# A fused gated-attention and feed-forward kernel: another order of its first loads, and one unit's transposes moved to the matrix engine

## The chip, the cores and the metric

The kernel runs on one core of a Trainium2 chip. Its engines work side by side, each through its own list of instructions in order: TensorE (PE in the profile; PEld is its weight load), VectorE (DVE), ScalarE (ACT), GpSimd (POOL) and SyncE (SP, which here only issues transfers). Transfers of all queues share 16 DMA engines. The metric is the device time of one execution in microseconds.

## The reference, cut to what matters

```python
B, H, S, D = q.shape                       # 4, 8, 768, 48
f = 1.0 / (1.0 + np.exp(-f_logit))
for t in range(S):
    state = f[:, :, t, :, None] * state + einsum('bhd,bhe->bhde', k[:, :, t], v[:, :, t])
    y[:, :, t] = einsum('bhd,bhde->bhe', q[:, :, t], state)
x = y.transpose(0, 2, 1, 3).reshape(B * S, H * D)      # 3072 x 384
h = x @ w_in                                            # w_in 384 x 2048
out = (0.5 * h * (1.0 + erf(h / sqrt(2)))) @ w_out      # w_out 2048 x 384
```

A recurrence with a decay for each channel is followed by a feed-forward layer with a gelu. Inputs and result are float32.

## The kernel before, in words

**Tiling.** The 3072 tokens are 24 tiles of 128. Two neighbouring tiles make a unit (u = 0 to 11, counted from zero: the "third unit" is u = 2, the "seventh" is u = 6) and also a group of the feed-forward part. Units 0 to 4 (`PAIRS`) hold tokens in an interleaved way and are called pair units; the others are natural ones.

**A unit's work.** Its logits (f), keys (k), values (v) and queries (q) are loaded by SyncE. ACT turns the logits to log decays (E at L494, L at L497), PE sums them over time (L521 to L527, L515), ACT takes exponentials of the sums (RG at L543, GT at L549, GL at L565 or L570), DVE or GpSimd multiplies keys and queries by them (L576), and the values are cast (VC, L583). Then keys and queries must be turned, that is transposed (`turn`, L592): either by PE with an identity matrix (L611) and a copy out of PSUM (L617), or, for units in `KDMA`, by two DMA transposes that SyncE issues (L599). PE makes the scores (L722 or L784), DVE masks them (L631), PE forms the state update (L745 or L806), which is carried on by DVE and GpSimd (L651 to L662), and the outputs (L699, L705, L758, L826). These are cast (L675) and turned (L691 or, for `XDMA`, by DMA at L679) to be the left side of the feed-forward part.

**A group's feed-forward work.** F1 (L875): eight steps of six matmuls of 256 columns with w_in, each step into one PSUM bank; ACT applies the gelu to each (L885). F2 (L896): for each tile 16 matmuls of 384 columns with w_out, in four quarters r = 0 to 3, each of which needs its piece of w_out and four of the group's gelu blocks; all 16 add up in one PSUM bank. The four banks of this pool (`s_fh`) serve F1 and F2 alike. A copy (L901) and a store (L906) follow; the last tile is split in halves (L917, L921).

**Weights.** w_in comes in three pieces, i0 (1024 columns, which steps 0 to 3 use), i1 (512, steps 4 and 5) and i2 (512, steps 6 and 7). w_out comes in four, o0 to o3, one for each quarter of F2. GpSimd issues them (L461, L464), as they are cast to bfloat16 on the way.

**Tables.** ACT holds one table for the exponentials and logarithms and another for the gelu. Each change loads a table (L953).

**Order.** Nothing in the order is left to a compiler. `Plan.run` lays all operations out with assumed durations; each has a priority, to which it adds a random number drawn from a seed of its unit (`SEEDS`). Every engine then runs its instructions in the planned order. The order of loads is the list `LOADS`. When the issuing engine changes from one entry to the next, a gate is put in: the transfer waits until an earlier one of the other kind has landed, the second back in the list for a SyncE load and the fourth back for a GpSimd load (or the next further back of that kind). The lines are

```python
        if i and order[i - 1][0] != eng:
            back = 4 if eng == "pool" else 2
            for j in range(i - back, -1, -1):
                if order[j][0] != eng:
                    gate = order[j][1]
                    break
```

While PE waits early in the plan, dummy matmuls on a tile of zeros fill the planned gaps (L947, junk).

Of the kernel before, what the change touches and what calls it, by code (L numbers as in the profile page):

```python
# [24 lines left out]

SPREAD, SEED = (1.0, 97)

SEEDS = [1643, 41, 3215, 1275, 2533, 2502, 823, 887, 1264, 763, 2447, 3095]

NUDGE = {}  # L30
XA = 0.0
# [53 lines left out]
class Plan:  # L85
# [30 lines left out]
    def run(self):  # L116
        free = dict.fromkeys(list(LAT), 0.7)
        free["DMA"] = 1.8
        rng = random.Random(SEED)
        own = [random.Random(x) for x in SEEDS]  # L120
        for o in self.ops:
            if o.prio > -5:
                k = min(max(int(o.prio % 1000) // 20, 0), len(SEEDS) - 1)
                o.prio += rng.uniform(-SPREAD, SPREAD)
                if SEEDS[k]:
                    w = (0.5, 1.0, 3.0, 8.0)[SEEDS[k] % 4]
                    o.prio += own[k].uniform(-w, w)
# [98 lines left out]
GAM = []  # L226
ODVE = [0, 1, 2, 4, 6, 7, 8, 9, 10, 11, 12, 13, 14, 16, 17, 18, 19, 20, 21, 22, 23]
XDMA = [5, 6, 7, 8, 9, 10, 11]
KDMA = [4, 5, 6, 7, 8, 9, 10, 11]
AJ = [2, 3, 4, 5, 6, 7, 8, 10, 11]  # L230
NGT = 4
GLD = []
G1D = [2, 3, 4]
YJ = [2, 3, 4]
ROWS = [16, 17, 18, 19]
AMX = []
WARM = 30.0
LOADS = ['f0', 'k0', 'v0', 'q0', 'f1', 'v1', 'k1', 'q1', 'i0', 'k2', 'f2', 'v2', 'q2', 'i1', 'i2', 'i3', 'o0', 'o1', 'o3', 'o2', 'f3', 'k3', 'q3', 'u4', 'v3']
LOADS += [f"u{n}" for n in range(12) if f"u{n}" not in LOADS and f"c{2 * n}" not in LOADS and f"f{n}" not in LOADS]


@with_exitstack
def kernel(
# [185 lines left out]
    wo_src = moe_w_out.rearrange("(r p j) m -> r p j m", r=4, j=4)  # L429
    for what in LOADS:  # L430
        m = int(what[1:])
# [160 lines left out]
    def turn(u, kq):  # L592


        for j in range(2):
            n = 2 * u + j
            sc = X[n]["sc"]
            if u in KDMA:
                P.add("DMA", 1.5, lambda sc=sc, j=j: nc.sync.dma_start_transpose(  # L599
# [256 lines left out]
    def ffn_group(g):  # L856
# [31 lines left out]
        for s_ in range(s):  # L888
# [14 lines left out]
            def store(n=n, osb=osb):  # L903
                w = C // 2 if n in ROWS else C
                for r in range(0, C, w):
                    nc.sync.dma_start(out=out[n * C + r:n * C + r + w, :], in_=osb.t()[r:r + w, :])  # L906
# [80 lines left out]
```

## Time and profile before

| | |
|---|---|
| Time, median of 3 runs | 182.77 us (182.22 to 183.18) |
| Span of the profiled run | 181.1 us |
| PE busy | 171.7 us, 95% |
| ACT busy | 125.2 us, 69%, of which 15 table loads take 19.2 |
| DVE busy | 96.3 us, 53% |
| GpSimd busy | 53.6 us, 30% |
| DMA | 32.61 MB, mean 180 GB/s |
| Largest groups | F1 (L875) 68.7 us, F2 (L896) 66.0, gelu (L885) 57.5 |

Busy time is the union of an engine's instructions. [...] Idle time of an engine matters only if the engine that sets the end waits for it.

### The profile page before, as it was taken

The numbers are of one execution on the slowest core, as the hardware profiler recorded it, in microseconds if no ns is written. First come the engines' busy times: TensorE is split into PE (matmuls) and PEld (weight loads), VectorE is DVE, ScalarE is ACT, GpSimd is POOL, SyncE is SP. The second block draws the span as 40 slices with busy tenths as digits, with TensorE's granted clock in tenths as the row PEclk, the third lists the DMA queues.
The fourth block names the chain that finished last, engine by engine and source line by source line (L and its number), as shares of the span: only waits on it lengthen the run. The fifth ranks groups of instructions, "written<-read, shape, count | busy, mean of one in ns | idle before, by whom it ended". The sixth has DMA issues, their size and how long they took to land.

```text
span 181.1 us, 4916 instructions
## 1 busy us (share of the span) xinstructions
PE 171.7 (95%) x1990; PEld 132.3 (73%) x1990; DVE 96.3 (53%) x194; ACT 125.2 (69%) x212; POOL 53.6 (30%) x116
## 2 busy tenths in 40 slices
PE   7788889999999999988999999999999999999993
PEld 2356669966787688785779689976697986886972
DVE  5289750058898564244896692527691625362110
ACT  2775198963899189999967759777585578560720
POOL 7657870003043641140176113112435110300000
PEclk9999999999999999999999999999999999999999
DMA  6999999949997898999999999999999872814102
GB/s 148 261 261 226 268 170 203 200 115 267 278 266 142 186 197 170 249 227 171 216 179 213 215 175 207 195 187 189 185 245 181 181 162 47 166 37 91 43 0 87
DMA packets 106998, 32.61 MB, mean 180 GB/s; under 512 B 102113, under 2 KB 106081, under 8 KB 106977
## 3 DMA queue, kind: packets, MB, share of 16 engines
q1 hardware_dynamic: 105056, 29.07, 79.7%
q0 software_dynamic: 1776, 3.15, 9.8%
q8 instruction: 15, 0.25, 0.6%
q10 hardware_dynamic: 144, 0.10, 0.2%
q14 instruction: 7, 0.05, 0.1%
HBM read 25.17 MB, written 4.72 MB: 165 GB/s over the span
## 4 chain that ended last, share of the span: by engine, by line
PE 64%; ACT 15%; DMA 15%; SPq 3%; issue 1%; DVE 0%; DVEq 0%
PE ps L875 26%; PE ps L896 25%; ACT gT L885 7%; DMA fl<-in_f_logit_dram 7%; DMA win<-in_moe_w_in_dram 5%; ACT L953 4%; SPq L449 3%; DMA kq<-sc 2%; PE ps L722 2%; PE ps L758 2%; PE ps L917 1%; ACT gt L549 1%; PE ps L521 1%; PE ps L699 1%; PE ps L745 1%
## 5 line engine op out<-in xcount | busy, mean ns | idle before, releaser
L885 ACT ACTIVATE gT<-ps 128x512 bf16<-128x512 f32 x96 | 57.5, 671 | 24.6 <-PE ps L875 23.0
L875 PE MATMUL ps<-xT,win 128*128 128x256 bf16 x576 | 68.7, 273 | 1.3 <-ACT gT L885 0.9
L896 PE MATMUL ps<-wout,gT 128*128 128x384 bf16 x368 | 66.0, 326 | 0.0
L875 PEld LDWEIGHTS <-win 128*128 128x128 bf16 x576 | 61.6, 114 | 3.9 <-issue 1.2
L896 PEld LDWEIGHTS <-gT 128*128 128x128 bf16 x368 | 34.2, 98 | 19.5
L583 POOL CAST vb<-vt 128x384 bf16<-128x384 f32 x22 | 12.6, 584 | 52.5 <-DMA vt<-in_v_dram 52.4
L631 DVE TENSOR_TENSOR am<-ps,mask 128x512 bf16<-128x512 f32 x28 | 17.6, 684 | 15.1 <-PE ps L722 15.1
L901 DVE COPY osb<-ps 128x384 f32<-128x384 f32 x20 | 11.1, 556 | 25.9 <-PE ps L896 18.2
L657 POOL TENSOR_TENSOR tn<-rr,gl 128x384 f32<-128x384 f32 x16 | 14.0, 872 | 35.2 <-DVE rr L655 34.6
L576 DVE TENSOR_TENSOR sc<-qt,gt 128x384 bf16<-128x384 f32 x23 | 14.0, 616 | 13.7 <-ACT gt L549 13.7
L576 DVE TENSOR_TENSOR sc<-kt,rg 128x384 bf16<-128x384 f32 x23 | 13.5, 597 | 11.3 <-ACT rg L543 11.3
L953 ACT ACT_TABLE_LOAD x15 | 19.2, 1283 | 0.3
L662 POOL CAST sb<-tn 48x192 bf16<-48x192 f32 x40 | 14.8, 371 | 11.6 <-DVE tn L651 6.6
L494 ACT ACTIVATE fl<-fl 128x768 f32<-128x768 f32 x12 | 10.1, 842 | 10.5 <-DMA fl<-in_f_logit_dram 10.5
L675 DVE CAST yb<-ps 128x384 bf16<-128x384 f32 x22 | 11.9, 555 | 7.4 <-PE ps L758 3.7
L631 DVE TENSOR_TENSOR am<-ps,maskp 128x512 bf16<-128x512 f32 x20 | 12.5, 684 | 2.2 <-PE ps L784 1.4
L543 ACT ACTIVATE rg<-ps 128x384 f32<-128x384 f32 x21 | 10.3, 503 | 4.4 <-PE ps L523 2.8
L549 ACT ACTIVATE gt<-ps 128x384 f32<-128x384 f32 x21 | 10.2, 503 | 3.9 <-PE ps L523 3.3
L947 PE MATMUL ps<-junk 128*128 128x512 bf16 (+3 forms) x36 | 10.4, 423 | 2.1 <-POOL junk L939 1.3
L655 DVE TENSOR_TENSOR rr<-ps,tn 128x384 f32<-128x384 f32 x16 | 8.9, 553 | 3.5 <-POOL tn L657 1.8
L497 ACT ACTIVATE lf<-fl 128x768 bf16<-128x768 f32 x12 | 10.1, 843 | 0.4
L947 PEld LDWEIGHTS <-junk 128*128 128x128 bf16 x36 | 3.6, 111 | 6.2 <-issue 3.5
(74 smaller groups left out, 130.4 us busy)
## 6 DMA issues: line engine op xcount, KB each, us to landing
out_dram<-osb SPq DMA_DIRECT2D x19, 192.0 KB, 3.1
fl<-in_f_logit_dram SPq DMA_DIRECT2D x14, 192.0 KB, 3.8
kt<-in_k_dram SPq DMA_DIRECT2D x14, 192.0 KB, 3.8
qt<-in_q_dram SPq DMA_DIRECT2D x14, 192.0 KB, 3.7
vt<-in_v_dram SPq DMA_DIRECT2D x14, 192.0 KB, 3.9
fl<-in_f_logit_dram SPq DMA_DIRECT2D x5, 384.0 KB, 6.2
kt<-in_k_dram SPq DMA_DIRECT2D x5, 384.0 KB, 6.2
vt<-in_v_dram SPq DMA_DIRECT2D x5, 384.0 KB, 5.7
```

The lines of the kernel that those rows point to most:

```text
L549: P.add("ACT", 0.40, lambda g=gps[j], gtv=gtv: nc.scalar.activation(gtv(), g.t()[:, 0:HD].rearrange("q (p h d) -> q p h d", h=2, d=D), AF. ...
L576: P.add("POOL" if pl else "DVE", 0.80 if pl else 0.475, lambda a=a, y=y, j=j, w=w, pl=pl, b=(gtv if w else rg): (nc.gpsimd if pl else nc.v ...
L583: P.add("ACT" if hv else "POOL", 0.40 if hv else 0.47, lambda y=y, j=j, hv=hv: (nc.scalar.copy if hv else nc.gpsimd.tensor_copy)(y["vb"].t ...
L631: P.add("POOL" if pl else "DVE", 1.15 if pl else 0.61, lambda hh=hh, pl=pl: (nc.gpsimd if pl else nc.vector).tensor_tensor(ams[hh].t(), ap ...
L657: P.add("POOL", 0.83, lambda: nc.gpsimd.tensor_tensor(tn.t(), rr.t(), glb(), ALU.mult), rd=[("rr", n), ("gl", n)], wr=[("tn", n)], bufs=[r ...
L662: P.add("POOL", 0.36, lambda hh=hh: nc.gpsimd.tensor_copy(sb.t()[64 * hh:64 * hh + D, :, D * hh:D * hh + D], tn.t()[64 * hh:64 * hh + D, : ...
L675: P.add("ACT" if help_ else "DVE", 0.40 if help_ else 0.475, lambda: copier(help_)(yb.t()[:, i, :], yp.t()[:, 0:HD]), rd=[("yp", n)], wr=[ ...
L875: nc.tensor.matmul(hps.t()[:, i * tok:(i + 1) * tok].rearrange("a (s t) -> a s t", s=s), col(fo)[:, kk, :], xT.t()[:, :, kk, :], start=(kk ...
L885: nc.scalar.activation(to, fr, AF.Gelu)
L896: nc.tensor.matmul(op.t()[:, 0:d_model], gT.t()[:, fo, s_ * C:(s_ + 1) * C], wout[fo // 4][:, fo % 4, :], start=(fo == 0), stop=(fo == FO ...
L947: nc.tensor.matmul(o.opens.t()[:, 0:w], junk[:, 0:C], junk[:, 0:w], start=True, stop=True, skip_group_check=True)
L953: nc.scalar.preload_act_table_set({"exp": "natural_log_exp_and_others", "gelu": "gelu_and_others"}[o.table])
```

## The change

Three lists of the schedule change and all seeds are drawn anew.

- `LOADS`: the third unit's logits (f2) go ahead of w_in; of w_in the last piece (i2) comes first, then i0, and i1 only after o0 and o1. By the rule of gates i2 then waits for v1, k2 for i2, and o0 for f2. Before, i0 waited for f1, i1 for k2, and k2 for nothing. (The entry i3 names no piece and does nothing.)
- `KDMA`: the seventh unit leaves the list, so PE turns it, with DVE's copies.
- `ROWS`: stores of tiles 14 and 15 are split in two halves.
- `SEEDS`: twelve new numbers.

It is meant to have the third unit's decays at hand before ACT turns to gelus, to let F1 start on a smaller piece of w_in, and to take a latency of two DMA transposes from the seventh unit.

```diff
-SEEDS = [1643, 41, 3215, 1275, 2533, 2502, 823, 887, 1264, 763, 2447, 3095]
+SEEDS = [2199, 3779, 3998, 3287, 1370, 1237, 3921, 2695, 3442, 2008, 790, 3051]
...
-KDMA = [4, 5, 6, 7, 8, 9, 10, 11]
+KDMA = [4, 5, 7, 8, 9, 10, 11]
...
-ROWS = [16, 17, 18, 19]
+ROWS = [14, 15, 16, 17, 18, 19]
...
-LOADS = ['f0', 'k0', 'v0', 'q0', 'f1', 'v1', 'k1', 'q1', 'i0', 'k2', 'f2', 'v2', 'q2', 'i1', 'i2', 'i3', 'o0', 'o1', 'o3', 'o2', 'f3', 'k3', 'q3', 'u4', 'v3']
+LOADS = ['f0', 'k0', 'v0', 'q0', 'f1', 'v1', 'k1', 'q1', 'f2', 'i2', 'i0', 'k2', 'v2', 'q2', 'i3', 'o0', 'o1', 'i1', 'o3', 'o2', 'f3', 'k3', 'q3', 'u4', 'v3']
```

## The prediction

> **What bounds the kernel now.** I read the page's busy line first, then busy time by stretch, the chain, and at last ACT and the DMA queues before 60 us.
>
> ```profile
> PE 171.7 (95%) x1990; PEld 132.3 (73%) x1990; DVE 96.3 (53%) x194; ACT 125.2 (69%) x212; POOL 53.6 (30%) x116
> ```
>
> PE is the bound, but a busy PE need not be a fast one, so I count its work. The chain gives prices where PE runs back to back:
>
> ```profile
> 97.55 0.55 PE ps L722 x16
> 108.62 5.89 PE ps L875 x54
> 119.23 3.90 PE ps L896 x24
> ```
>
> A logit-side product of the feed-forward part (F1, L875) costs 5.89/54 = 0.109 us, one of its second half (F2, L896) 3.90/24 = 0.1625, a natural unit's scores (L722) 0.55. The busy time by stretch gives the room:
>
> ```profile
> 20.60:28.60 8.00, 7.13 (x105) 5.98 (x106) 3.37 (x7) 5.51 (x7) 5.28 (x10) 1.00 1.14 198
> 28.60:50.00 21.40, 21.40 (x261) 16.41 (x259) 10.34 (x21) 16.36 (x28) 1.50 (x3) 1.00 0.99 215
> 50.00:60.00 10.00, 9.55 (x167) 7.96 (x166) 8.31 (x16) 9.30 (x18) 4.83 (x9) 1.00 0.86 197
> 75.00:85.00 10.00, 9.06 (x81) 6.72 (x80) 4.09 (x8) 9.93 (x17) 2.64 (x5) 1.00 1.14 209
> 85.00:178.10 93.10, 93.06 (x962) 74.33 (x960) 49.10 (x90) 62.18 (x111) 20.22 (x37) 1.00 0.81 156
> ```
>
> Columns: length, then busy us and count of PE, PEld, DVE, ACT, POOL. The same view for single lines gives counts to multiply:
> - 20.6 to 28.6: 36 F1 = 3.9, attention pieces of the chain 2.0, together 5.9 of 8.0: 2.1 us of slack (1.13 of it is filled by five junk matmuls, L947).
> - 50 to 60: 48 F1 = 5.2, 7 F2 = 1.1, attention 2.7: 9.0 of 10, slack 1.0.
> - 75 to 85: 36 F1 = 3.9, 25 F2 = 4.1, scores and state 0.7: 8.7 of 10, slack 1.3. ACT is full there (9.93).
> - 85 to 178.1: 336 F1 = 36.6, 246 F2 = 40.0, the split last tile (L917) 2.65, attention 12.5: 91.8 of 93.1.
>
> So the second half is packed: added PE work lengthens it, and only slack before 85 us can be won, some 4.4 us. Where it comes from:
>
> ```profile
> 10.84 9.78 DMA win<-in_moe_w_in_dram
> 20.67 2.16 PE ps L875 x18
> 28.86 7.43 ACT gT L885 x12
> 36.31 1.28 ACT L953
> 40.33 6.34 DMA fl<-in_f_logit_dram
> 52.96 1.28 ACT L953
> ```
>
> F1 starts when the first w_in piece lands (20.6). From 25.6 to 36.3 ACT does 16 gelus; only after a table change at 36.31 does it make unit 2's exponentials. Unit 3 and 4 then wait for loads that SyncE issues from 37.75 on, as it waits for w_out (o3): 16.8 us in the waits of SP. The DMA view of 35.5 to 38.5 has only 0.15 MB in 3 us.
>
> ```profile
> 22.56 0.84 ACT L494 ACTIVATE fl<-fl 128x768 f32<-128x768 f32 x1 [3.89 <-DMA fl<-in_f_logit_dram]
> 24.30 1.28 ACT L953 ACT_TABLE_LOAD   x1
> 37.60 0.49 ACT L549 ACTIVATE gt<-ps 128x384 f32<-128x384 f32 x1
> ```
>
> Unit 2's logits came at 22.5, 10.8 us after issue. In the DMA view of 15 to 19 the reason stands:
>
> ```profile
> q0 software_dynamic: 340, 0.68, 90.1%
> q1 hardware_dynamic: 370, 0.14, 20.0%
> ```
>
> While weights flow (q0), 170 KB/us are theirs and 35 are left to the inputs (q1), which alone get 1.31 MB in 5 us = 262 KB/us (8 to 13).
>
> **What the Trainium skill says.** "DMA: Bandwidth & Descriptors", section Queues, rings and completion order: an engine turns between its queues packet by packet. That agrees: about equal counts (340, 370), so the queue with bigger packets takes the bandwidth. "ScalarE: Activation LUTs", section What ACT_TABLE_LOAD costs: 1283 ns for any set, and a drain of 1380 more. The trace has 1283 each, 15 times; the drain isn't seen (the load at 24.30 ends 0.01 before the gelu). "TensorE: Matmul & The Clock Gate", Part 4: a 128x128 bf16 transpose takes some 275 ns in context, and needs a copy from PSUM. Here it takes 219 (L611), pipelined: eight weight loads in 0.45 us.
>
> **The change, part by part.**
>
> *Loads.* Nothing is added or dropped; order and gates change. The first w_in transfer (now i2, 384 KB) waits for v1 rather than f1. f1 landed at 10.55; 384 KB at 262 KB/us is 1.5 us, so v1 is at 12.1, q1 at 15.0. Before, i0 was issued at 10.84 and, by 0.1 MB outside 15 to 19, began to flow at about 14.3: 3.5 later. So i2 flows from 15.6 (estimate). By then f2, now behind q1, has 0.6 us x 262 = 157 KB; 227 are left. At 35 KB/us that ends after the whole of i2 and i0 (1152 KB, 6.4 us at 180), at 22; with twice that share while i2 flows (its packets are half as long) it lands at 20.4. Bounds: 16.5 (no contention) and 22.5. I take 20.4, only 2 us earlier than before. i2 lands about 18.8, i0 about 23.2 (before 20.6).
>
> The sense of it is on ACT: unit 2's E and L (1.7), sums (0.7), exponentials (1.9, from 37.6 to 39.4 plus a wait for the subtraction) can all precede the gelus, then one table load 1.28: gelus start at 20.4 + 5.6 = 26.0 against 25.6. PE in 18 to 26 has 12 F1 from i2 and 12 from i0 until its four PSUM banks are full, as before. So +0.4; the junk block of 1.13 us need not recur, take -0.4: sum 0. With the bounds -2.0 (f2 at 18) and +2 (f2 at 22.5).
>
> A pair of table loads goes (36.31, and one around it): 2.6 us of ACT, worth something only where ACT limits.
>
> *Added waits.* k2 on SP now waits for i2 (18.8), with v2 and q2 queued behind it. o0 on GpSimd waits for f2; behind it stand o1, i1, then unit 1's state work and unit 2's v casts. After 22 the inputs get some 262 KB/us for a microsecond and then a trickle under o0, o1, i1 (1152 KB, to about 29): q2 lands near 31.5 rather than 25.7. Its products ran at 38.1 to 39.1, so this lateness is hidden by the gelus. Unit 2 then turns near 32 to 34, 5 us earlier. i1 at about 30 feeds the last F1 of both groups while 12 gelus are still to do: hidden. F2 needs o2 at the end of its sum, about 38.5 (before 39.5); meanwhile 36 F1, early F2 quarters and unit 2 keep PE full.
>
> o3 follows the v casts: about 36.3, so f3 goes out 1 to 1.5 us sooner, and unit 2's tokens are at hand for F1 by 43 rather than 51. Hence the slack of 50 to 60 should go: -1.0. That of 75 to 85 (ACT full, a key transpose by DMA awaited at 83.4 and 84.1) should shrink by most: -1.2, bounds 0 and -1.3.
>
> *Seventh unit by TensorE.* Removes 2 of 16 DMA transposes (1.25 us of SP issue and 3.4 to landing each) and adds 16 transposes on PE: 16/8 x 0.45 = 0.9 us, and two DVE copies of 0.68. DVE is 84% busy in 90 to 100 but has 40 us to spare after it; its copies lie beside F1 and F2. PE is packed there: +0.9 in full. Before, unit 6's scores (97.55) met no wait of PE, so little comes back. SP is free 2.5 us sooner for loads: hidden.
>
> *Rows and seeds.* Stores of tiles 14 and 15 in halves: two more issues near 125 us, out of buffers' way, 0. The seeds reshuffle priorities in every unit. They alter no work; where PE is packed, order costs nothing. Their part is in the slack before 85: no price in the trace, I take 0, bounds +-1.
>
> Sum: 0 - 1.0 - 1.2 + 0.9 = -1.3: 182.8 - 1.3 = 181.5.
>
> **Rivals.**
> - *Slower, weights starve the rest.* f2 lands at 22.5 as now; five microseconds of exponentials stand before the first gelu, so gelus start at 28. PE loses about 1.3 of its 5.9 us of work before 28.6; unit 6 adds 0.9; the later slack shrinks by only 0.3: 182.8 + 1.9 = 184.7. For it: the 170 to 35 split, and weights that come as one queue. Against it: f2 has a head start, and PE had F1 to do.
> - *No change.* Only one of the two later slacks goes (-1.0), against 0.9: 182.7. For it: the packed second half makes unit 6's cost sure.
> - *Much faster.* f2 is through before the weights flow (18 or less), gelus start at 23.6, two more microseconds are won in the first stretch: 179.5. Against it: my 227 KB left at 15.6.
>
> **How the numbers follow.** Forecast 181.5 (0.42), much faster 179.5 (0.13), no change 182.7 (0.17), slower 184.7 (0.28). The limit of 0.5% is 0.9 us: faster, below 181.9, takes the first two, 0.55; same 0.17; slower, above 183.7, 0.28. The range leaves out a tenth at each side: 179.4 (half of much faster) to 184.9 (the starved case with a further loss by seeds left out).
>
> **What would show it.** Right: 14 or fewer table loads; no exponentials of unit 2 after the first gelus; f2's activation before 21.5; gelus from about 26; PE's count in 50 to 60 and 75 to 85 up by a microsecond of work; L611 at 80 instructions; SP's transposes of kq at 14. Wrong: gelus from 28 or later; a PE gap between 20 and 30 of over 3 us; f3 issued after 38; scores of unit 6 waiting for a DVE copy; a stretch after 85 with PE under 99%.

## The result, and the profile after

The changed kernel takes 189.5 us (median of 6 runs, 188.46 to 191.29) against 182.63: 1.0368 times as long, 95% interval 1.0315 to 1.0421. Some executions of a kernel fall in a slower state (one of these six, 191.29): the ratios, and the times in the table of experiments, leave them out. The span of the profiled run grew from 181.1 to 187.7 us. The page's busy line of PE and the group of table loads, after:

```profile
PE 174.6 (93%) x2002; PEld 133.9 (71%) x2002; DVE 100.2 (53%) x196; ACT 130.7 (70%) x216; POOL 52.6 (28%) x116
L953 ACT ACT_TABLE_LOAD x19 | 24.4, 1283 | 0.3
```

PE is busy for a smaller share, and table loads rose from 15 to 19 where 14 or fewer were forecast. Busy time by stretch, after (length, then PE, PEld, DVE, ACT, POOL, the granted PE clock, DMA share, GB/s; the granted clock is the share of its full speed at which PE was allowed to run):

```profile
20.00:25.00 5.00, 5.00 (x88) 3.19 (x88) 3.74 (x7) 2.05 (x4) 3.48 (x8) 0.89 1.09 220
25.00:30.00 5.00, 2.64 (x50) 2.09 (x46) 1.31 (x3) 4.20 (x7) 0.00 (x0) 1.00 1.13 214
30.00:35.00 5.00, 3.12 (x20) 2.52 (x21) 2.58 (x6) 1.20 (x2) 1.17 (x2) 0.66 0.38 100
35.00:40.00 5.00, 5.00 (x79) 4.18 (x77) 1.85 (x3) 3.55 (x6) 2.55 (x5) 1.00 0.17 17
...
85.00:184.50 99.50, 99.49 (x1012) 79.26 (x1009) 50.55 (x90) 72.38 (x122) 20.71 (x39) 1.00 0.78 152
```

The same view of the kernel before:

```profile
20.00:25.00 5.00, 4.64 (x81) 3.85 (x80) 2.93 (x6) 2.39 (x3) 4.33 (x9) 1.00 1.13 231
25.00:30.00 5.00, 4.21 (x42) 3.54 (x40) 1.04 (x3) 4.25 (x7) 1.49 (x3) 1.00 1.14 182
30.00:35.00 5.00, 5.00 (x49) 5.00 (x47) 0.00 (x0) 5.00 (x10) 0.00 (x0) 1.00 1.08 212
35.00:40.00 5.00, 5.00 (x39) 3.29 (x38) 1.88 (x4) 4.33 (x9) 0.00 (x0) 1.00 0.44 94
```

From 85 us on PE is packed in both. Before, 93.1 us of work were left there, after 99.5. So 6.4 of the 6.6 us of span had been lost by then: by the forecast's price 0.9 of it is unit 6's added work, and some 5.5 us is work that PE did not do before 85 (30 more F1 and 16 more F2 stand behind it, 5.9 us at 0.109 and 0.1625 each). In 20 to 25 PE is busy all the time, but 2.32 us of it are dummy matmuls (L947): only 12 F1 are done by 25, against 24 before. In 25 to 35 PE was busy 5.76 us against 9.21, and part of that ran at a granted clock of 0.66. The chain of waits of the changed kernel names what it stood for:

```profile
12.33 6.93 DMA win<-in_moe_w_in_dram
19.28 11.96 DMA kt<-in_k_dram
31.26 0.57 DVE sc L576
31.88 0.61 PE ps L611 x4
32.48 1.28 PE ps L875 x6
34.19 1.67 PE ps L875 x12
```

Unit 2's keys (k2) went out at 19.28, when i2 had landed, and took 12 us to land, that is to be there in full. The F1 steps behind them are slow as well: 1.28 us for 6 and 1.67 for 12, against 0.65 and 1.31 at 0.109 each, so 1.0 us more. The timeline of the changed kernel shows who stood still:

```profile
16.49 0.84 ACT L494 ACTIVATE fl<-fl 128x768 f32<-128x768 f32 x1
18.66 0.83 POOL L657 TENSOR_TENSOR tn<-rr,gl 128x384 f32<-128x384 f32 x1 [1.90 <-DVE rr L655]
19.43 1.15 POOL L464 DMA_DIRECT2D wout<-in_moe_w_out_dram  x2
22.44 0.84 PE L875 MATMUL ps<-xT,win 128*128 128x256 bf16 x6
27.64 1.91 ACT L885 ACTIVATE gT<-ps 128x512 bf16<-128x512 f32 x3
31.26 0.56 DVE L576 TENSOR_TENSOR sc<-kt,rg 128x384 bf16<-128x384 f32 x1 [4.66 <-DMA kt<-in_k_dram]
31.74 0.62 DVE L694 COPY xT<-ps 128x384 bf16<-128x384 bf16 x2
31.88 0.61 PE L611 MATMUL ps<-ident,sc 128*128 128x128 bf16 x4 [4.23 <-DVE sc L576]
33.80 2.85 ACT L885 ACTIVATE gT<-ps 128x512 bf16<-128x512 f32 x4 [4.25 <-PE ps L875]
37.12 0.83 POOL L657 TENSOR_TENSOR tn<-rr,gl 128x384 f32<-128x384 f32 x1 [3.49 <-DVE rr L655]
37.90 0.60 POOL L464 DMA_DIRECT2D wout<-in_moe_w_out_dram  x1
42.26 0.37 SPq L449 DMA_DIRECT2D fl<-in_f_logit_dram  x1
```

Four steps of F1 fill the four banks, then PE's list has a key transpose, and PE waits 4.23 us. ACT finishes its three gelus and waits as long. On DVE even group 1's left side (xT at 31.74), long ready, stands behind the key product. On GpSimd o3 comes only after unit 2's state step (37.12), and f3, whose gate it is, leaves at 42.26 rather than 37.75. The DMA view of the changed kernel, first for 16 to 21 us, then for 21 to 23, then for 33 to 39 (q0 carries the weights, q1 the inputs):

```profile
q0 software_dynamic: 652, 1.01, 114.7%
q1 hardware_dynamic: 3, 0.00, 0.1%
...
kt<-in_k_dram SPq DMA_DIRECT2D x1, 384.0 KB, 12.0
```

```profile
q1 hardware_dynamic: 836, 0.32, 59.1%
q0 software_dynamic: 83, 0.18, 51.0%
```

```profile
DMA packets 7, 0.02 MB, mean 3 GB/s; under 512 B 6, under 2 KB 6, under 8 KB 6
```

First weights alone flow while k2 waits for i2. Then the inputs move 0.32 MB in two microseconds (k2 has 0.39), until o0, o1 and i1, issued from 19.4 on, take most of the bandwidth: 0.97 MB against 0.23 of inputs in 23 to 29. k2's transfer reports sixteen completions: ten came by 23.9 us, the other six between 27.2 and 31.24, and its readers wait for the last. Why some parts lag so far stays open. At 33 to 39 the DMA engines rest, with w_out half loaded.

### The profile page after: what moved, and what is told of

It reads as the page before. It is cut to its first block, busy times and chain, and to the rows that moved or that the text cites. A ratio compares the mean times of both kernels' runs of the same rounds, so it can differ in the third digit from the quotient of the medians.

```text
span 187.7 us, 4945 instructions
## 1 busy us (share of the span) xinstructions
PE 174.6 (93%) x2002; PEld 133.9 (71%) x2002; DVE 100.2 (53%) x196; ACT 130.7 (70%) x216; POOL 52.6 (28%) x116
## 4 chain that ended last, share of the span: by engine, by line
PE 75%; DMA 12%; DVE 5%; ACT 4%; issue 1%; POOL 1%; DVEq 0%
PE ps L875 31%; PE ps L896 31%; DMA kt<-in_k_dram 6%; DMA win<-in_moe_w_in_dram 4%; DVE sc L576 3%; PE ps L722 2%; DMA fl<-in_f_logit_dram 2%; PE ps L758 2%; PE ps L917 1%; PE ps L611 1%; PE ps L699 1%; PE ps L521 1%; ACT rg L543 1%; PE ps L745 1%; ACT gt L549 1%
## 5 line engine op out<-in xcount | busy, mean ns | idle before, releaser
L885 ACT ACTIVATE gT<-ps 128x512 bf16<-128x512 f32 x96 | 58.0, 666 | 22.7 <-PE ps L875 21.1
L875 PE MATMUL ps<-xT,win 128*128 128x256 bf16 x576 | 71.2, 276 | 0.6 <-ACT gT L885 0.6
L576 DVE TENSOR_TENSOR sc<-kt,rg 128x384 bf16<-128x384 f32 x23 | 16.8, 741 | 15.3 <-ACT rg L543 10.6
L953 ACT ACT_TABLE_LOAD x19 | 24.4, 1283 | 0.3
L662 POOL CAST sb<-tn 48x192 bf16<-48x192 f32 x40 | 14.3, 359 | 21.2 <-DVE tn L651 15.2
L576 DVE TENSOR_TENSOR sc<-qt,gt 128x384 bf16<-128x384 f32 x23 | 13.5, 595 | 5.2 <-ACT gt L549 4.4
L611 PE MATMUL ps<-ident,sc 128*128 128x128 bf16 x80 | 8.0, 243 | 5.0 <-DVE sc L576 5.0
L947 PE MATMUL ps<-junk 128*128 128x512 bf16 (+3 forms) x32 | 9.7, 438 | 1.3 <-POOL junk L939 1.3
L611 PEld LDWEIGHTS <-sc 128*128 128x128 bf16 x80 | 6.0, 110 | 6.9 <-DVE sc L576 6.4
```

Source lines behind the costliest of these rows:

```text
L576: P.add("POOL" if pl else "DVE", 0.80 if pl else 0.475, lambda a=a, y=y, j=j, w=w, pl=pl, b=(gtv if w else rg): (nc.gpsimd if pl else nc.v ...
L611: nc.tensor.transpose(tpv()[:, i, p, :], sc.t()[:, i, 2 * p:2 * p + 2, :], ident)
L662: P.add("POOL", 0.36, lambda hh=hh: nc.gpsimd.tensor_copy(sb.t()[64 * hh:64 * hh + D, :, D * hh:D * hh + D], tn.t()[64 * hh:64 * hh + D, : ...
L875: nc.tensor.matmul(hps.t()[:, i * tok:(i + 1) * tok].rearrange("a (s t) -> a s t", s=s), col(fo)[:, kk, :], xT.t()[:, :, kk, :], start=(kk ...
L885: nc.scalar.activation(to, fr, AF.Gelu)
L953: nc.scalar.preload_act_table_set({"exp": "natural_log_exp_and_others", "gelu": "gelu_and_others"}[o.table])
```

## The experiments

Two kinds were made. Four kernels take one of the lists or the seeds alone, so that the whole order is planned anew. The others keep the planned order of every engine but for what the edit names. A name with b is the kernel before with an edit, one with a the changed kernel with an edit. Times are medians; ratios are to the kernel before on the same chip. a_k2free turned out to be the changed kernel itself, so it serves to compare with on its chip, which it shares with a_wlate, a_o3early and a_u6dma; there the kernel before took 182.06 us.

| run | us | ratio, 95% interval |
|---|---|---|
| b_loads | 199.98 | 1.0994, 1.0965 to 1.1022 |
| b_seeds | 199.06 | 1.0923, 1.0896 to 1.0951 |
| b_kdma | 193.4 | 1.065, 1.0599 to 1.07 |
| a_loads | 206.07 | 1.1313, 1.1289 to 1.1338 |
| a_k2free | 189.47 | 1.0414, 1.0365 to 1.0464 |
| a_wlate | 184.3 | 1.0126, 1.0076 to 1.0176 |
| a_o3early | 186.5 | 1.0243, 1.0223 to 1.0264 |
| a_u6dma | 190.93 | 1.0459, 1.0424 to 1.0494 |
| a_k2only | 187.8 | 1.0322, 1.0269 to 1.0376 |
| a_wlate_k2 | 183.85 | 1.0093, 1.006 to 1.0126 |
| a_pelate | 189.28 | 1.0383, 1.0348 to 1.0418 |
| a_warm | 188.65 | 1.0352, 1.0279 to 1.0425 |
| a_pedve | 189.78 | 1.0412, 1.0388 to 1.0436 |
| a_o0first | 183.77 | 1.0099, 1.0073 to 1.0126 |
| b_f3free | 182.4 | 1.003, 1.0016 to 1.0044 |
| b_f3o1 | 182.19 | 1.0004, 0.9991 to 1.0017 |
| a_wk_u6x2 | 185.96 | 1.0187, 1.0158 to 1.0217 |
| a_wk_rows | 184.44 | 1.0118, 1.0099 to 1.0137 |

### One part at a time, planned anew

The kernel before with the new `LOADS`, the new `SEEDS` or the new `KDMA` alone, and the changed kernel with the old `LOADS`:

```diff
-SEEDS = [1643, 41, 3215, ...]
+SEEDS = [2199, 3779, 3998, ...]
```

> Theory L (the new order of loads makes the loss, by k2 behind i2 and the weights): 186 to 189 us, a PE gap of 3 us or more near 27 to 32. Rival P (the seeds' order and unit 6 on PE make it): 182 to 184 us. In a re-planned kernel the seeds' numbers meet another order, so 1 us either way says nothing.

> Theory L: 182 to 185 us, since only priorities move and PE after 85 us is packed. Rival P: 186 us or more.

> Theory L: before plus the 0.9 us of sixteen transposes, 183 to 184 us. Rival P: more than 185 us, with scores of unit 6 late and a stretch after 85 us with PE under 99%. Should PE's transposes be hidden: 182.6.

> The changed kernel with the old order of loads alone. Theory L: 183 to 185 us (what is left is unit 6's 0.9 us and the seeds). Rival P: 188 us or more.

All four came out slower than both kernels, by 11 to 24 us over the one before. Neither theory gave a reason for that size. Three of the times lie in the open ranges of rival P (b_seeds, b_kdma, a_loads), but b_loads is far above both theories, so the four don't decide between them. Busy time by stretch of the kernel with the new seeds alone, and PE's own waits in 80 to 130 us:

```profile
80.00:100.00 20.00, 15.32 (x155) 10.45 (x152) 10.99 (x21) 17.90 (x33) 4.69 (x9) 0.97 0.99 203
100.00:120.00 20.00, 17.74 (x215) 13.81 (x214) 15.74 (x27) 10.51 (x16) 6.40 (x12) 0.86 0.88 169
```

```profile
PE ps L745 <- DVE sc L576: 4.9, 4, 2.3
PE ps L875 <- ACT gT L885: 2.4, 2, 1.4
```

Where the kernel before has 19.53 and 20.00 us of PE in these two stretches, this one has 15.32 and 17.74. A packed PE is thus a property of the old order, and the new seeds cost some 17 us with lists that they were not drawn for. A part of the change can't be priced by putting it alone into such a plan. Still, one thing can be read: PE's gap before 35 us came only with the new loads (13.41 us busy in 20 to 40 for b_loads, 18.32 for b_seeds, 18.68 for b_kdma and 18.07 for a_loads, 18.85 before).

### The order kept: k2 and the weights

```diff
-            if gate is not None:
+            if gate is not None and name != "k2":
```

> The changed kernel, every engine's order kept; only k2's gate on i2 is gone, so k2, v2 and q2 are queued from about 12 us on. Theory G (PE's gap at 27 is the wait for k2): the wait for k2 goes, but v2 and q2 still share with the weights, so a shorter gap of 1 to 2 us before the state matmuls: 185 to 187 us. Rival S (the loss lies in the seeds' order, the gap would be filled or made elsewhere): 188.5 to 190 us.

The loads are named kt2, not k2, so this edit changed nothing (k2 was issued at 19.27, in the changed kernel at 19.28). The run repeats the changed kernel: 189.47 against 189.5. With the right name:

```diff
-            if gate is not None:
+            if gate is not None and name != "kt2":
```

> The changed kernel, every order kept; the gate of k2 on i2 is gone (the run before under the name of k2's release left the gate in place, as the transfer is called kt2). k2, v2, q2 are queued from 12 us. Theory G: k2 lands before 26, PE's gap at 27 falls from over 4 us to under 2; the weights still starve v2 and q2: 185 to 187.5 us. Rival S: 188.5 us or more.

A miss: k2 was issued at 11.53 and its last part still came only at 28.7, beside weights most of the way. The median is 1.7 us lower, but the interval overlaps the changed kernel's (1.0315 to 1.0421), so no gain is shown. The gate is a small part of the lateness. Next, all five later weight issues go behind the casts of unit 2's values, where the kernel before had most of them:

```diff
     P.run()
+    late = [o for o in P.placed if o.name in ('io0', 'io1', 'ii1', 'io3', 'io2')]
+    P.placed = [o for o in P.placed if o not in late]
+    at = max(i for i, o in enumerate(P.placed) if o.name == 'VC5') + 1
+    P.placed[at:at] = late
```

> The changed kernel with the issues of o0, o1, i1, o3, o2 all moved behind the casts of unit 2's values in GpSimd's list, nothing else moved. Theory G: k2 lands before 25, no gap at 27, f3 leaves about 38 instead of 42: 183 to 185 us, if i1 (about 35) is not waited for. Rival S: 188 us or more. Rival W (early w_out is what F2 needs): a new wait of PE for w_in or w_out of 2 us or more, 186 to 188 us.

Here 5.2 us came back, of the 7.4 by which the changed kernel is slower on this chip (189.47 against 182.06). k2 landed at 24.4, f3 left at 39.6. Two things besides k2 have a share that no run separates: the edit also sends o3 and o2 ahead of unit 2's state step, and the mean granted clock was 1.000 in all four executions, against 0.982 to 0.989 in those of a_k2free. Against the changed kernel's one execution at 0.991 (188.46) the gain is 4.2 us. The rival on early w_out was right on its wait, but not on the time: PE's first F2 waited for o0, which landed at 33.5.

```profile
33.49 0.82 PE L896 MATMUL ps<-wout,gT 128*128 128x384 bf16 x4 [2.00 <-DMA wout<-in_moe_w_out_dram]
```

Both edits together:

> Both edits: the five weight issues behind the casts of v2, and k2 without its gate. If the wait for o0 (33.5 us) is what is left of the loss in the run with late weights, v2 and so o0 come 2 to 3 us sooner and the time is 181.5 to 183 us. If k2, v2, q2 now delay w_in (i0 after 25): 184 us or more.

183.85 lies between the two forecasts, and the interval overlaps that of late weights alone. Its timeline and its busy time by stretch:

```profile
25.64 0.39 PE L611 MATMUL ps<-ident,sc 128*128 128x128 bf16 x4
31.99 0.82 PE L896 MATMUL ps<-wout,gT 128*128 128x384 bf16 x4 [0.74 <-DMA wout<-in_moe_w_out_dram]
```

```profile
25.00:30.00 5.00, 4.45 (x50) 4.04 (x48) 2.77 (x7) 4.99 (x8) 3.66 (x7) 1.00 0.44 80
30.00:35.00 5.00, 4.26 (x68) 3.46 (x66) 2.24 (x5) 2.49 (x5) 1.77 (x4) 1.00 1.11 193
```

The key transpose runs at 25.64 instead of 31.88, and PE's 8.71 us in 25 to 35 are near the 9.21 of before. Keeping o0 early (the same edits, with o0 left in its place) moved the wait rather than removing it, as k2 came at 26.5:

> k2 without its gate, and of the five weight issues only o1, i1, o3, o2 behind the casts; o0 keeps its early place. If what is left of the loss with late weights is PE's wait for o0 at 31: 182.5 to 183.5 us. If o0's 384 KB ahead of unit 2's inputs delay k2 past 26: 184.5 us or more.

183.77, so neither of its two forecasts. The second mechanism alone, o3 and o2 ahead of unit 2's state step:

```diff
+    late = [o for o in P.placed if o.name in ('io3', 'io2')]
...
+    at = max(i for i, o in enumerate(P.placed) if o.name == 'VC5') + 1
```

> The changed kernel with the issues of o3 and o2 moved ahead of unit 2's state step on GpSimd, right behind the casts. Theory H (the DMA pause of 33 to 39 us, and so the late o2 and f3, costs a part): f3 leaves at about 38, 187 to 188 us, PE's gap at 27 unchanged. If the gap alone counts: 189 to 190 us.

f3 left at 37.4, and k2 still landed at 30.6. Two executions took 186.5 us, 3.0 less than a_k2free. But these two had a mean granted clock of 0.991, at which the changed kernel has 188.46, so 2.0 less. Two more took 189.7 and 190.2 at 0.982, where a_k2free has 188.8 to 190.8. So the rest of the DMA engines at 33 to 39 seems to cost 2 to 3 us, but that stands on two executions. As a_wlate contains this edit, the share of the earlier keys in its 5.2 us may be no more than half.

### The order kept: who stands behind the keys

In the first run only PE's list was changed: the key transposes and state products of unit 2 behind four F1 steps. In it unit 2's state step read its bank ahead of those products, so the carried state is another one; only its waits are read. In the second run the key products on DVE, and all that reads them, moved too.

```diff
+        (late if i < to and (o.name in ('KP4', 'KP5', 'Tk4', 'Tk5', 'S2') or late and hit) else keep).append(o)
...
+    at = min(i for i, o in enumerate(keep) if o.name == 'Tq4')
+    P.placed = keep[:at] + late + keep[at:]
```

> The changed kernel with PE's first two key transposes and the state products of unit 2 moved behind four steps of F1 in PE's list; no transfer and no gate is changed, k2 still lands at 31. Theory G (an in-order list stands behind the wait): F1 fills the gap, 185 to 187 us. If the late keys themselves cost the time (unit 2's chain sets the end): 189 us or more.

> The changed kernel; unit 2's key products on DVE, its key transposes and state products on PE and what reads these are moved behind, just ahead of its query transposes; no transfer moves. In the run with PE's list alone changed, group 1's left side stood on DVE behind the key product (copies at about 32), so F1 could not go on. Theory G2 (both lists stand behind k2, the late keys cost little by themselves): copies at about 27, the gap under 1.5 us, 185 to 187 us. If unit 2's chain itself sets the end: 188.5 us or more.

The second run did not help (189.78). With PE's list alone changed, F1 soon stood for group 1's left side on DVE. With both lists changed, the timeline of PE shows the wait handed on:

```profile
26.78 2.13 PE L875 MATMUL ps<-xT,win 128*128 128x256 bf16 x18 [0.78 <-ACT gT L885]
30.98 0.86 PE L611 MATMUL ps<-ident,sc 128*128 128x128 bf16 x8 [1.15 <-DVE sc L576]
33.04 0.20 PE L806 MATMUL ps<-vb,sc 64*128 64x96 bf16 x1 [1.20 <-POOL vb L583]
```

F1 did run in the old gap, but then PE waited for the keys, the values (landed at 32.4) and the queries (33.6) one after the other. So the theory that only the head of a list was at fault fell, as far as this place in the order goes: the lateness of all three inputs costs, unless work that needs none of them is put into the whole stretch. That was not tried.

Twenty dummy matmuls in the gap kept PE at a granted clock of 1.00 in 30 to 35 us:

```diff
+            if o.name == "F1.0.3":
+                tk = [x for x in P.placed if x.name == "Tk4"][0]
+                for _ in range(20):
+                    nc.tensor.matmul(tk.opens.t(), junk[:, 0:C], junk, start=True, stop=True, skip_group_check=True)
```

> The changed kernel with twenty more matmuls on zeros (some 4.3 us) ahead of the first key transpose, so that PE is busy while it waits for k2. If the lower granted clock after the gap (0.5 to 0.66 in 30 to 35 us) costs time by itself: 187.5 to 188.8 us. If the clock costs nothing: 189 to 190; if the dummies outlast the wait, more.

188.65 is where a cost of the clock was expected, but its interval contains the changed kernel's ratio. Its four executions lie from 187.35 to 190.08, the slowest at a mean clock of 1.000. Whether the slower clock costs its microsecond stays open.

### The order kept: the seventh unit and the stores

Unit 6 back to DMA transposes at the places of its copies:

```diff
-            P.add("PE", 0.225, lambda trans=trans: trans(0), rd=[("kp", n), "ident"], wr=[("tk", n)],
+            P.add("PE", 0.225, lambda trans=trans: None if u == 6 else trans(0), rd=[("kp", n), "ident"], wr=[("tk", n)],
...
+                kq.t()[:, :, :, j, :].rearrange("a i p t -> a (i p) t"), sc.t().rearrange("p i h d -> p (i h d)")) if u == 6 else copier(help_)(
```

> The changed kernel with unit 6 turned by DMA again at the same places of the order (no PE transposes of unit 6). By the price of 0.9 us: 188.4 to 188.8 us. If its work on PE was hidden: 189.5. If the latency of the DMA is exposed at this place: over 190 us, with unit 6's scores waiting for kq.

No gain: 190.93 against 189.47 for the changed kernel on this chip, with intervals that overlap. The profiled execution took 194.3 us, more than the median, so only the place of its wait is read, in the waits of 90 to 105 us:

```profile
PEld L723 <- DMA kq<-sc: 2.3, 1, 2.3
PE ps L723 <- DMA kq<-sc: 2.1, 1, 2.1
```

(L723 is L722 moved by a line.) In this order the scores follow too soon for a transfer, so the run takes one cost away and adds another, and does not price PE's transposes. Their own price was then sought by making each twice, and the halved stores by making them whole, both on the version with late weights and ungated k2:

```diff
-                for p in range(P2):
+                for p in list(range(P2)) * (2 if u == 6 else 1):
```

> The version with late weights and k2 ungated (ratio 1.0093 to before); each of unit 6's sixteen transposes on PE is made twice, the output is the same. By the forecast's price of 0.9 us for sixteen: ratio 1.014, some 184.7 us. If PE had room there: 1.009. If the second DVE copy's wait or the PSUM bank counts too: over 1.017.

> The same version with the stores of tiles 14 and 15 whole again, every order kept. The forecast's price for the halves is 0: ratio 1.008 to 1.011, as without the edit.

The doubled transposes add 0.9 us to PE's busy time in that group of records (0.61, 0.39 and 0.39 become 1.06, 0.61 and 0.61) and 0.0069 to 0.0094 of 182.3 to the time, 1.3 to 1.7 us, against the two runs without them, whose intervals make the difference uncertain by about 0.7. The ratio of 1.0187 lies where more than PE's own work was expected to count. The price of 0.9 is not excluded, but it stands at the low end. The stores made no difference that these intervals can show.

### The kernel before: is its slack to be had?

f3 without its gate, or with its gate on o1:

```diff
+                g = [x for _, x in order if x.name == "o1"][0] if name == "fl3" else gate
```

> The kernel before, every order kept; f3's gate on o3 is gone, so f3, k3, q3 are queued from 21 us, next to the weights. If the pause of the DMA engines at 35 to 38 us costs through units 3 and 4: 181 to 182 us. If the inputs slow the weights that F2 waits for: over 183 us. If the slack before 60 us is not set by these loads: 182 to 182.6.

> The kernel before, every order kept; f3 waits for o1 (35.8 us) rather than o3 (37.7), so it fills the pause of the DMA engines without meeting most of the weights. If units 3 and 4 are held by their loads: 181.2 to 182.2 us; else 182 to 182.6.

With the gate on o1, f3 left at 34.47 instead of 37.75. The timeline of SP (its lines are one further down) and the busy time of 50 to 60:

```profile
34.47 0.37 SPq L450 DMA_DIRECT2D fl<-in_f_logit_dram  x1
```

```profile
50.00:60.00 10.00, 9.56 (x169) 8.06 (x167) 8.31 (x15) 9.17 (x17) 4.29 (x10) 1.00 0.79 161
```

PE's 9.56 us are the 9.55 of before, and the time is the same. Loads that are issued three microseconds sooner win nothing while the order stays. Without any gate it was slower by 0.3%.

## Why the prediction was wrong

**The step that failed** is the one under added waits: that q2's "lateness is hidden by the gelus", because unit 2's products had run at 38. That was their place in the old order, in which the keys' product stands behind that of the queries:

```profile
38.12 0.56 DVE L576 TENSOR_TENSOR sc<-qt,gt 128x384 bf16<-128x384 f32 x1 [11.87 <-ACT gt L549]
38.60 0.55 DVE L576 TENSOR_TENSOR sc<-kt,rg 128x384 bf16<-128x384 f32 x1
```

The new order puts key products and transposes right behind four F1 steps, on DVE and on PE, and both engines wait for k2 until 31.2. The forecast gave no landing for k2 at all. Putting the weights behind the values takes k2 to 24.4 and returns 5.2 of 7.4 us: shown for the weights' place as a whole, not for k2 alone. That the readers' new place is at fault is read from the waits; an order with other work in the whole stretch was not tried.

**The transfers** went much as forecast. The inputs had their burst (0.32 MB in 21 to 23), then a trickle, and q2 landed at 33.6 (forecast 31.5). Not foreseen was that the last part of k2 would come with that trickle, at 31.24, though ten of its sixteen parts were there by 23.9.

**The landing of f2** was mis-sized at 20.4; it landed at 16.47, the bound for no contention. The 227 KB that were to be left when i2 flows were counted from landing times, though the transfer's last bytes come sooner. The sum was off as well: at its own 70 KB/us (twice 35), 227 KB from 15.6 on are through by 18.8. The early f2 opened o0's gate at 16.5, but o0 left only at 19.43, behind a state step of unit 1 (18.66), where the forecast had all of that work after it. So the place in GpSimd's list set the time, not the gate.

**F1 on the smaller piece**: i2 landed at 19.26 (forecast 18.8), but the first F1 ran at 22.44 (before 20.67), since dummy matmuls and unit 1's scores stand ahead of it in PE's list. The profiled execution ran them at a granted clock of 0.50 (17.7 to 21.1). In the profile of a_k2only the clock is 1.00 there, and F1 starts at 20.57. In the changed kernel PE waits for k2 after this all the same.

**The unit's exponentials** did come before the first gelu, as forecast, and gelus started at 27.64 (forecast 26.0); without that slow stretch, in a_k2only, at 25.76. The rival "much faster" asked for f2 by 18. It came by then, and the gelus still did not start at 23.6, as ACT stood behind a copy of unit 1's transposes and then behind its sums, for 2.08 and 2.65 us. And the saving of a pair of table loads was not one: 19 loads against 15, so later parts of the new order turn more often.

**f3** was to leave at 36.3 and left at 42.26, since o3 stood behind unit 2's state step. That seems to cost 2 to 3 us, on two executions. It too follows from unit 2's late inputs: o3 stands behind the casts, and GpSimd waited 8.73 us for v2.

**The slack of 50 to 60 and 75 to 85** was counted as won, -2.2 us. In the kernel before, earlier loads alone win none of it: the first of the two is not set by the transfers. In the changed kernel PE was busy 34.27 of the 35 us from 50 to 85, against 33.61, only 0.7 us more. This term had no ground in the profile, which showed that PE had slack, not that the loads set it.

**Seventh unit, 0.9 us**: not excluded by the doubled transposes, which point to 1.3 to 1.7; not measured in the changed kernel itself. **Stores, 0**: nothing seen. **Seeds, 0 with 1 us either way**: wrong as a statement on order (17 us alone). In the changed kernel they fit their lists, and PE is packed after 85 us as before.

**The rival of starved weights** (184.7) had the right side and named the weights, but expected the wait at f2; it came at k2, and was larger. Once the weights wait and k2 goes early, 1.5 us remain over the kernel before: unit 6's 0.9 and PE's wait for o0 (0.7 in the timeline) are of that size, though no run took both away.

## What to carry to other kernels

Where engines run fixed lists, a transfer that comes late costs what stands behind its first reader in every list, so look for that reader in the new order, not in the old one. Before bulk transfers are put earlier in a list, ask which inputs they will share the DMA engines with: here 1.1 MB of weights, issued from 19.4 on, met the inputs that PE needed next. And slack on the bounding engine is a gain only if the trace shows what sets it.

## What the runs showed of the hardware that was not expected

- With k2 queued beside the weights from 11.5 us on (a_k2only), the two queues moved about equal counts of packets in 16 to 22 us. So the inputs got 42 KB/us, where alone they move 262. Fifteen of k2's sixteen parts were there by 23.7, and its readers waited for the last until 28.7.

```profile
q0 software_dynamic: 642, 1.00, 91.3%
q1 hardware_dynamic: 641, 0.25, 22.9%
```

- After PE's gap the granted clock was 0.66 in 30 to 35 us, and F1 took up to 0.213 us a matmul instead of 0.109. With dummies in the gap it was 1.00.
